# Router logits of a fused attention and expert kernel: from split float32r matmuls to float32 matmuls in four column groups, and four gathers issued in two steps

## The chip, the cores and the metric

One core of a Trainium2 chip runs the whole kernel in one launch. Its engines are TensorE (PE, with its weight loads shown as PEld), VectorE (DVE), ScalarE (ACT), GpSimd (POOL) and SyncE (SP, which issues most DMAs). The metric is device time in microseconds.

## The reference, cut to what matters

```python
scores = scale * np.matmul(q, k.transpose(0, 1, 3, 2))     # 4 batches, 8 heads, 576 places, 64 wide
scores = np.where(masks, scores, -1e9)                      # heads 0-3 a local band, 4-7 every 32nd place
attn = np.exp(scores - scores.max(-1)); attn /= attn.sum(-1) + 1e-9
x = (attn @ v).transpose(0, 2, 1, 3).reshape(2304, 512)
logits = x @ w_gate + modality_bias[modality_id]            # 8 experts
e_idx = np.argmax(logits, axis=1); gate_w = softmax(logits)[e_idx]
for e in range(8):                                          # each token goes to one expert
    out[e_idx == e] = gate_w * (np.maximum(x[e_idx == e] @ w1[e], 0) @ w2[e])
h = out @ w_in; g = np.where(h > 0, h, np.exp(np.minimum(h, 0)) - 1)
result = g @ w_out
```

The logits decide by argmax where a token goes, so they are computed to float32 accuracy. The matmuls of the two feed-forward stages split each operand into a high and a low part in float32r and add three products.

## The kernel before, in words

The kernel has three stages. Attention takes the first 130 us or so, the expert stage follows, and the dense stage (`w_in`, `w_out`) fills the rest. The order of the instructions on every engine is the order in which the code emits them.

**Attention** runs over 32 steps `n` (`NU`): 4 batches by 4 pairs of heads (`PAIRS = [2, 3, 0, 1]`) by 2 halves. A step of the loop emits work of several steps, so that the engines overlap: the scores of step n (`emit_S`, matmul at L1027, two heads in two row groups of 64 rows of the array), transposes of q and k (`emit_T`, L1002), the transposed probabilities of step n-2 (`emit_PT`, L1053), the values of step n-3 (`emit_PV`, L1084, one float32 matmul per piece), the transposed result of step n-5 (`emit_X`, L1121), and the exponentials of step n-1 on ACT (`emit_exp`, L1045). For the masks DVE reads the scores out of PSUM (L1033 or L1038) and takes the row maximum; POOL subtracts the maximum (L1041); then ACT can take the exponentials. The two score banks of PSUM (tag "S") are used again in the next step, so PE's scores of step n+1 wait for DVE's masks of step n.

**The logits.** `emit_X` puts x^T into SBUF in two float32r tiles: ACT casts the high part `xh` (L1129), DVE subtracts it from the PSUM tile for the low part `xl` (L1132). The weight `wgs` holds the high and low parts of `w_gate` side by side, 16 columns (L975, L976). Once all four pairs of a half batch are there, `emit_L` multiplies its 288 places: 4 pieces of the contraction, each with `xh` and with `xl`, eight matmuls of 128 by 16 weights and 288 columns (L1141, L1142) into one bank. There are eight such blocks, six in the attention loop and two in the expert stage. `emit_lg` turns the 16 rows of logits back to places on partitions by nine PE transposes (L1148), and DVE adds the bias and the two halves (L1149, L1150). It runs twice: for the first half of the places in step 21, for the second half in the expert stage. The bias itself is made in step 14 by `emit_bias`: PE transposes the modality numbers, DVE copies them (`m1`, L982; `m0`, L983), POOL forms the bias (L985 to L987), and then `router.constants()` emits a dozen small POOL instructions (iotas, memsets and selects, L214 to L227).

**The first job.** Once the first half of the logits is known, a background generator (`early`) picks the fullest expert among the first 1,152 places, makes a table of its rows and starts its job while attention still runs. The loop calls `bg()` at points between DVE's instructions; a yield of `STEP` holds the generator until the loop's next step. One of its pieces issues four gathers (L460), indirect DMAs on the POOL queue that fetch 128 rows of x each; `scale` (L464) and `trans` (L475) use them some steps later.

Of the kernel before, what the change touches and what calls it, by code (L numbers as in the profile page):

```python
# [8 lines left out]
F32 = mybir.dt.float32  # L9
F32R = mybir.dt.float32r  # L10
# [405 lines left out]
def ffn(tc, ctx, x_dram, part_dram, ident, router, conv, bank, w1, w2, out, run_attention):  # L416
# [187 lines left out]
    def early():  # L604
        STEP = Background.STEP
        yield from router.choose(0, NE)
        yield STEP
        yield from router.early(r_p, lambda: fetch_to(0), lambda: fetch_to(1))
        for c in range(4):
            gather(jobs[0], c)  # L610
            yield STEP if c == 3 else None
        split_to(0)
        fetch_to(2)
        yield STEP
        split_to(1)
        fetch_to(3)
        yield
        for c in range(4):
            scale(jobs[0], c)
            yield STEP if c % 2 else None  # L620
        for kk in range(2):
            trans(jobs[0], kk)
            yield STEP
# [236 lines left out]
def attention(tc, bg, q, k, v, mod, mbias, wg, x_dram, ident, router, bank):  # L860
# [97 lines left out]


    wgf = const.tile([128, 4, E], F32, name="wgf")  # L960
    wgs = const.tile([128, 4, 2 * E], F32R, name="wgs")
    mi = const.tile([NT, 128, 2], I32, name="mi")
    mf = const.tile([NT, 128], F32, name="mf")
    bb = const.tile([128, 2, E], F32, name="bb")
# [1 line left out]
    m0 = const.tile([128, NT], F32, name="m0")  # L966
    bias = const.tile([128, NT, E], F32, name="bias")
    bt = const.tile([128, NT, E], F32, name="bt")
    def load_router():
        nc.scalar.dma_start(wgf, wg.rearrange("(k p) e -> p k e", p=128))  # L970
        nc.scalar.dma_start(mi, mod.bitcast(I32).rearrange("(i p two) -> i p two", p=128, two=2))
        nc.scalar.dma_start(bb, mbias.rearrange("m e -> (m e)").partition_broadcast(128).rearrange("p (m e) -> p m e", m=2))

    def emit_wgs():
        nc.scalar.copy(wgs[:, :, 0:E], wgf)  # L975
        nc.vector.tensor_tensor(wgs[:, :, E:2 * E], wgf, wgs[:, :, 0:E].bitcast(F32), ALU.subtract)  # L976
        nc.vector.tensor_copy(mf, mi[:, :, 0])

    def emit_bias():
# [5 lines left out]
        nc.gpsimd.tensor_tensor(bt, m0.unsqueeze(2).to_broadcast(sh), bb[:, 0:1].to_broadcast(sh), ALU.mult)  # L985
        nc.gpsimd.tensor_tensor(bias, m1.unsqueeze(2).to_broadcast(sh), bb[:, 1:2].to_broadcast(sh), ALU.mult)
        nc.gpsimd.tensor_tensor(bias, bias, bt, ALU.add)  # L987
        router.constants()

    st = {}  # L990
# [65 lines left out]

    xs, stores = {}, []

    xh, xl = (xt_p.tile([128, 4, S], F32R, name=nm) for nm in ("xh", "xl"))
    lgt = const.tile([2 * E, 2 * S], F32, name="lgt")  # L1060

    def emit_PV(n):
        b, pr, s = steps[n]
# [50 lines left out]
    def emit_X(n):  # L1114
# [11 lines left out]
                return t.rearrange("p (m a) -> p a m", a=G)[:, 4 * s:4 * s + 4]  # L1126
            return t.rearrange("p (i m) -> p i m", m=m)[:, nj * s:nj * s + nj]

        nc.scalar.copy(view(xh), ps)  # L1129
        while stores:  # L1130
            stores.pop()(nc.scalar if n + LX < NU else nc.sync)
        nc.vector.tensor_tensor(view(xl), ps, view(xh).bitcast(F32), ALU.subtract)  # L1132
        bg()
        bg()

    def emit_L(b, half):

        ps = bank("T", "ps_l", 2 * E, S // 2)
        c = slice(half * (S // 2), (half + 1) * (S // 2))
        for j, kk in enumerate(PAIRS):  # L1140
            nc.tensor.matmul(ps, lhsT=wgs[:, kk], rhs=xh[:, kk, c], start=j == 0, stop=False)  # L1141
            nc.tensor.matmul(ps, lhsT=wgs[:, kk], rhs=xl[:, kk, c], start=False, stop=j == 3)  # L1142
        nc.scalar.copy(lgt[:, b % 2 * S + c.start:b % 2 * S + c.stop], ps)

    def emit_lg(i0, i1):
        ps = bank("T", "ps_g", 128, i1 - i0, 2 * E)
        for i in range(i0, i1):
            nc.tensor.transpose(ps[:, i - i0], lgt[:, i % NE * 128:(i % NE + 1) * 128], ident[0:2 * E, 0:2 * E])  # L1148
        nc.vector.tensor_tensor(lg[:, i0:i1], ps[:, :, 0:E], bias[:, i0:i1], ALU.add)  # L1149
        nc.vector.tensor_tensor(lg[:, i0:i1], lg[:, i0:i1], ps[:, :, E:2 * E], ALU.add)  # L1150

    for j in range(4):
        emit_T(0, j)
# [67 lines left out]
```

## Time and profile before

| | |
|---|---|
| median of 3 runs | 785.39 us (781.82 to 787.17) |
| the profiled execution's own time | 784.26 us |
| its span, first to last instruction | 782.5 us |
| PE busy | 762.0 us, 97% of the span |
| DVE, ACT, POOL busy | 509.4, 395.9, 103.2 us |
| mean granted TensorE clock | 0.998 |

A busy time counts an instruction from its start to its end, and overlapping matmuls once. The end of a matmul is modelled, so that in a run of matmuls one starts well before the end that is shown for the one before it, and the difference of two starts tells what a matmul costs. In a timeline, consecutive instructions of the same kind are merged into a row with their count; the row's duration reaches from the first start to the last end. A bracket shows idle time of the engine ahead of the row and what ended it. A float32 matmul stands in the trace as two matmul records (two passes over the moving columns), a transpose or a float32r matmul as one.

### The profile page before, as it was taken

To read this page: it belongs to the slowest core of one execution; us is meant where nothing else is said; L and a number is where in the kernel's file an instruction comes from. 1 tells how busy PE (TensorE), PEld (TensorE's weight loads), DVE (VectorE), ACT (ScalarE), POOL (GpSimd) and SP (SyncE) were. 2 spreads that over 40 slices of the span, in tenths; PEclk is the share of its full clock that TensorE was granted. 3 is DMA by queue.
4 is the path that set the end of the run, shared out by engine and by line. 5 is a ranking of instruction groups with operands and counts; after the bars stand their busy time and mean duration, and the time that the engine had idled before them with its cause. 6 is when DMAs were issued, how large, how long until landed. Compare 5 with 4: busy or idle time off the path is not lost.

```text
span 782.5 us, 12469 instructions
## 1 busy us (share of the span) xinstructions
PE 762.0 (97%) x4513; PEld 634.9 (81%) x4513; DVE 509.4 (65%) x1122; ACT 395.9 (51%) x759; POOL 103.2 (13%) x131
## 2 busy tenths in 40 slices
PE   7999989999999999999999999999999999999995
PEld 6999877888888888888787888888888888888885
DVE  4688898776879777677477565664565454545453
ACT  4567566424444444545466455555465444444342
POOL 4335352121020010000000000001010020101011
PEclk9999999999999999999999999999999999999999
DMA  7887591456475666553422221113132030201111
GB/s 162 176 197 179 125 247 58 138 163 204 162 265 171 205 232 199 184 185 118 124 95 91 85 95 41 52 57 121 40 127 89 0 108 1 94 14 52 56 41 67
DMA packets 100300, 94.35 MB, mean 121 GB/s; under 512 B 45433, under 2 KB 78731, under 8 KB 100235
## 3 DMA queue, kind: packets, MB, share of 16 engines
q1 hardware_dynamic: 90880, 74.66, 32.7%
q0 software_dynamic: 4480, 14.68, 5.3%
q10 hardware_dynamic: 4875, 4.17, 1.9%
q8 instruction: 37, 0.61, 0.3%
q14 instruction: 28, 0.23, 0.1%
HBM read 70.95 MB, written 22.54 MB: 119 GB/s over the span
## 4 chain that ended last, share of the span: by engine, by line
PE 44%; DVE 4%; ACT 3%; issue 0%; POOLq 0%; POOL 0%; DVEq 0%; ACTq 0%
PE o_ps L819 8%; PE o_ps L820 7%; PE o_ps L821 7%; PE h_ps L732 7%; PE h_ps L731 7%; PE h_ps L733 7%; DVE r L796 1%; DVE t L795 1%; DVE wl L481 1%; ACT gh L797 1%; ACT wh L480 1%; ACT t L792 0%; ACT e L793 0%; DVE cv_r L158 0%; ACT cv_a L146 0%
## 5 line engine op out<-in xcount | busy, mean ns | idle before, releaser
L795 DVE SCALAR_TENSOR_TENSOR t<-e,t 128x512 f32<-128x512 f32 (+1 forms) x80 | 51.1, 639 | 112.7 <-ACT e L793 112.6
L731 PE MATMUL h_ps<-xh,wh 128*128 128x512 f32 (+1 forms) x320 | 118.6, 371 | 1.3 <-PEq L745 1.3
L732 PE MATMUL h_ps<-xl,wh 128*128 128x512 f32 (+1 forms) x320 | 118.6, 371 | 0.2 <-DVE xl L469 0.2
L733 PE MATMUL h_ps<-xh,wl 128*128 128x512 f32 (+1 forms) x320 | 118.6, 370 | 0.0
L819 PE MATMUL o_ps<-wh,gh 128*128 128x512 f32 x288 | 113.4, 394 | 0.7 <-ACT o L828 0.5
L821 PE MATMUL o_ps<-wh,gl 128*128 128x512 f32 x288 | 113.0, 392 | 0.0
L820 PE MATMUL o_ps<-wl,gh 128*128 128x512 f32 x288 | 112.9, 392 | 0.0
L792 ACT ACTIVATE t<-h_ps 128x512 f32<-128x512 f32 (+1 forms) x80 | 44.2, 553 | 102.2 <-PE h_ps L733 95.4
L797 ACT CAST gh<-r 128x512 fp32r<-128x512 f32 (+1 forms) x80 | 46.2, 577 | 81.0 <-DVE r L796 81.0
L798 DVE TENSOR_TENSOR gl<-r,gh 128x512 fp32r<-128x512 f32 (+1 forms) x80 | 51.2, 640 | 51.4 <-ACT gh L797 51.4
L481 DVE TENSOR_TENSOR wl<-wraw,wh 128x1024 fp32r<-128x1024 f32 x56 | 68.6, 1224 | 14.3 <-ACT wh L480 12.7
L731 PEld LDWEIGHTS h_ps<-xh,wh 128*128 128x128 f32 x320 | 60.2, 188 | 13.4 <-issue 1.7
L732 PEld LDWEIGHTS h_ps<-xl,wh 128*128 128x128 f32 x320 | 60.3, 188 | 12.4 <-DVE xl L469 0.6
L733 PEld LDWEIGHTS h_ps<-xh,wl 128*128 128x128 f32 x320 | 60.1, 188 | 10.9
L819 PEld LDWEIGHTS o_ps<-wh,gh 128*128 128x128 f32 x288 | 54.2, 188 | 13.6 <-ACT o L828 0.9
L516 PE MATMUL y_ps<-hh,wh 128*128 128x512 f32 x160 | 64.2, 401 | 0.0
L821 PEld LDWEIGHTS o_ps<-wh,gl 128*128 128x128 f32 x288 | 54.0, 188 | 12.5 <-DVE gl L798 0.4
L497 PE MATMUL h_ps<-xh,wh 128*128 128x512 f32 x160 | 63.6, 398 | 0.0
L820 PEld LDWEIGHTS o_ps<-wl,gh 128*128 128x128 f32 x288 | 54.1, 188 | 11.1
L499 PE MATMUL h_ps<-xh,wl 128*128 128x512 f32 x160 | 62.9, 393 | 0.0
L518 PE MATMUL y_ps<-hh,wl 128*128 128x512 f32 x160 | 62.8, 393 | 0.0
L498 PE MATMUL h_ps<-xl,wh 128*128 128x512 f32 x160 | 62.8, 392 | 0.0
(180 smaller groups left out, 1380.9 us busy)
## 6 DMA issues: line engine op xcount, KB each, us to landing
wraw<-in_moe_w_dram SPq DMA_DIRECT2D x80, 256.0 KB
raw<-in_moe_w_in_dram SPq DMA_DIRECT2D x16, 512.0 KB
raw<-in_moe_w_out_dram SPq DMA_DIRECT2D x16, 512.0 KB
w_f<-cv_r SPq DMA_DIRECT2D x32, 256.0 KB
wraw<-w_f SPq DMA_DIRECT2D x16, 512.0 KB
part_dram<-o POOLq DMA_DIRECT2D x18, 256.0 KB, 2.9
part<-part_dram SPq DMA_DIRECT2D x18, 256.0 KB
qn<-in_q_dram SPq DMA_DIRECT2D x8, 288.0 KB
```

The lines of the kernel that those rows point to most:

```text
L481: nc.vector.tensor_tensor(WL[i], raw, WH[i].bitcast(F32), ALU.subtract)
L497: nc.tensor.matmul(ps, lhsT=a, rhs=job.xh[kk], start=kk == 0, stop=False)
L498: nc.tensor.matmul(ps, lhsT=a, rhs=job.xl[kk], start=False, stop=False)
L499: nc.tensor.matmul(ps, lhsT=b, rhs=job.xh[kk], start=False, stop=kk == 3)
L516: nc.tensor.matmul(ps, lhsT=a, rhs=hh, start=f == 0, stop=False)
L518: nc.tensor.matmul(ps, lhsT=b, rhs=hh, start=False, stop=f == NCH - 1)
L731: nc.tensor.matmul(ps[:, 0:n], lhsT=a, rhs=yh, start=kk == 0, stop=False)
L732: nc.tensor.matmul(ps[:, 0:n], lhsT=a, rhs=yl, start=False, stop=False)
L733: nc.tensor.matmul(ps[:, 0:n], lhsT=b, rhs=yh, start=False, stop=kk == 3)
L819: nc.tensor.matmul(ps, lhsT=a, rhs=WH[i][:, 512:1024], start=first, stop=False)
L820: nc.tensor.matmul(ps, lhsT=a, rhs=WL[i][:, 512:1024], start=False, stop=False)
L821: nc.tensor.matmul(ps, lhsT=b, rhs=WH[i][:, 512:1024], start=False, stop=last)
```

## The change

The logits are multiplied in float32. `emit_X` copies x^T once, unsplit, to `xt`; `xl` and its subtraction are gone. The weight `wgs` is now 32 columns wide, `w_gate` four times side by side, written by four POOL copies. `emit_L` issues four matmuls, one per piece of the contraction, each to another group of 32 PSUM partitions (another group of 32 columns of the array), so the four partial sums stay apart; ACT copies 128 rows in place of 16. `emit_lg` adds the four up: nine float32 matmuls whose weights are 128 by 128 pieces of the copied logits and whose moving operand is a small constant `sel` (128 by 8, a one where the partition number modulo 32 is the expert's). DVE's second addition (L1150) is gone. `sel` is made in `emit_bias`, by a POOL iota and three DVE instructions, ahead of `router.constants()`. In `early` the step now ends after the second gather in place of the fourth.

```diff
--- before.py
+++ after.py
@@ -608,7 +608,7 @@
         yield from router.early(r_p, lambda: fetch_to(0), lambda: fetch_to(1))
         for c in range(4):
             gather(jobs[0], c)
-            yield STEP if c == 3 else None
+            yield STEP if c == 1 else None
         split_to(0)
         fetch_to(2)
         yield STEP
@@ -958,7 +958,7 @@
 
 
     wgf = const.tile([128, 4, E], F32, name="wgf")
-    wgs = const.tile([128, 4, 2 * E], F32R, name="wgs")
+    wgs = const.tile([128, 4, 32], F32, name="wgs")
     mi = const.tile([NT, 128, 2], I32, name="mi")
     mf = const.tile([NT, 128], F32, name="mf")
     bb = const.tile([128, 2, E], F32, name="bb")
@@ -966,14 +966,16 @@
     m0 = const.tile([128, NT], F32, name="m0")
     bias = const.tile([128, NT, E], F32, name="bias")
     bt = const.tile([128, NT, E], F32, name="bt")
+    sel_i = const.tile([128, E], I32, name="sel_i")
+    sel = const.tile([128, E], F32, name="sel")
     def load_router():
         nc.scalar.dma_start(wgf, wg.rearrange("(k p) e -> p k e", p=128))
         nc.scalar.dma_start(mi, mod.bitcast(I32).rearrange("(i p two) -> i p two", p=128, two=2))
         nc.scalar.dma_start(bb, mbias.rearrange("m e -> (m e)").partition_broadcast(128).rearrange("p (m e) -> p m e", m=2))
 
     def emit_wgs():
-        nc.scalar.copy(wgs[:, :, 0:E], wgf)
-        nc.vector.tensor_tensor(wgs[:, :, E:2 * E], wgf, wgs[:, :, 0:E].bitcast(F32), ALU.subtract)
+        for i in range(32 // E):
+            nc.gpsimd.tensor_copy(wgs[:, :, i * E:i * E + E], wgf)
         nc.vector.tensor_copy(mf, mi[:, :, 0])
 
     def emit_bias():
@@ -985,6 +987,11 @@
         nc.gpsimd.tensor_tensor(bt, m0.unsqueeze(2).to_broadcast(sh), bb[:, 0:1].to_broadcast(sh), ALU.mult)
         nc.gpsimd.tensor_tensor(bias, m1.unsqueeze(2).to_broadcast(sh), bb[:, 1:2].to_broadcast(sh), ALU.mult)
         nc.gpsimd.tensor_tensor(bias, bias, bt, ALU.add)
+
+        nc.gpsimd.iota(sel_i, pattern=[[-1, E]], base=32, channel_multiplier=1)
+        nc.vector.tensor_scalar(sel_i, sel_i, 31, None, ALU.bitwise_and)
+        nc.vector.tensor_copy(sel, sel_i)
+        nc.vector.tensor_scalar(sel, sel, 0.0, None, ALU.is_equal)
         router.constants()
 
     st = {}
@@ -1056,8 +1063,8 @@
 
     xs, stores = {}, []
 
-    xh, xl = (xt_p.tile([128, 4, S], F32R, name=nm) for nm in ("xh", "xl"))
-    lgt = const.tile([2 * E, 2 * S], F32, name="lgt")
+    xt = xt_p.tile([128, 4, S], F32, name="xt")
+    lgt = const.tile([128, 2 * S], F32, name="lgt")
 
     def emit_PV(n):
         b, pr, s = steps[n]
@@ -1126,28 +1133,26 @@
                 return t.rearrange("p (m a) -> p a m", a=G)[:, 4 * s:4 * s + 4]
             return t.rearrange("p (i m) -> p i m", m=m)[:, nj * s:nj * s + nj]
 
-        nc.scalar.copy(view(xh), ps)
+        nc.scalar.copy(view(xt), ps)
         while stores:
             stores.pop()(nc.scalar if n + LX < NU else nc.sync)
-        nc.vector.tensor_tensor(view(xl), ps, view(xh).bitcast(F32), ALU.subtract)
         bg()
         bg()
 
     def emit_L(b, half):
 
-        ps = bank("T", "ps_l", 2 * E, S // 2)
+        ps = bank("T", "ps_l", 128, S // 2)
         c = slice(half * (S // 2), (half + 1) * (S // 2))
         for j, kk in enumerate(PAIRS):
-            nc.tensor.matmul(ps, lhsT=wgs[:, kk], rhs=xh[:, kk, c], start=j == 0, stop=False)
-            nc.tensor.matmul(ps, lhsT=wgs[:, kk], rhs=xl[:, kk, c], start=False, stop=j == 3)
+            o = 32 * (j % 4)
+            nc.tensor.matmul(ps[o:o + 32], lhsT=wgs[:, kk], rhs=xt[:, kk, c], start=j < 4, stop=j >= 4 - 4)
         nc.scalar.copy(lgt[:, b % 2 * S + c.start:b % 2 * S + c.stop], ps)
 
     def emit_lg(i0, i1):
-        ps = bank("T", "ps_g", 128, i1 - i0, 2 * E)
+        ps = bank("T", "ps_g", 128, i1 - i0, E)
         for i in range(i0, i1):
-            nc.tensor.transpose(ps[:, i - i0], lgt[:, i % NE * 128:(i % NE + 1) * 128], ident[0:2 * E, 0:2 * E])
-        nc.vector.tensor_tensor(lg[:, i0:i1], ps[:, :, 0:E], bias[:, i0:i1], ALU.add)
-        nc.vector.tensor_tensor(lg[:, i0:i1], lg[:, i0:i1], ps[:, :, E:2 * E], ALU.add)
+            nc.tensor.matmul(ps[:, i - i0], lhsT=lgt[:, i % NE * 128:(i % NE + 1) * 128], rhs=sel, start=True, stop=True)
+        nc.vector.tensor_tensor(lg[:, i0:i1], ps, bias[:, i0:i1], ALU.add)
 
     for j in range(4):
         emit_T(0, j)
```

On DVE, at the end of step 14 and the first rows of step 15, before (the maxima and values of step 11, the modality numbers, then the masks of step 15):

```order
L1092 RECIPROCAL rs<-rs 72x8 [waits DVE_49]
L1097 TENSOR_TENSOR xs<-ps_v,rs 72x2x128 [waits DVE_49]
L1097 TENSOR_TENSOR xs<-ps_v,rs 72x2x128
L982 COPY m_223<-pm 128x18 [waits PE_49]
L983 TENSOR_SCALAR m_224<-m_223 128x18 [waits DVE_49]
L1038 ISA sm,mx<-ps_sc_1160,mask_l 96x128 [waits PE_49,Pool_49]
L1038 ISA mx 96x1
```

and now:

```order
L1099 RECIPROCAL rs<-rs 72x8 [waits DVE_49]
L1104 TENSOR_TENSOR xs<-ps_v,rs 72x2x128 [waits DVE_49]
L1104 TENSOR_TENSOR xs<-ps_v,rs 72x2x128
L984 COPY m_223<-pm 128x18 [waits PE_49]
L985 TENSOR_SCALAR m_224<-m_223 128x18 [waits DVE_49]
L992 TENSOR_SCALAR sel_i<-sel_i 128x8 [waits Pool_49]
L993 CAST sel<-sel_i 128x8 [waits DVE_49]
L994 TENSOR_SCALAR sel<-sel 128x8 [waits DVE_49]
L1045 ISA sm,mx<-ps_sc_1149,mask_l 96x128 [waits PE_49,Activation_49]
L1045 ISA mx 96x1
```

Three instructions for `sel` now stand between the modality numbers and the masks, and the first of them waits for POOL's iota, which stands behind the three bias instructions on POOL.

On POOL, around step 27 (`sm` is the subtraction of the maximum, `xg` a gather of the first job), before:

```order
L1041 TENSOR_TENSOR sm<-sm,mx 72x576
L400 TENSOR_TENSOR A<-oa,vals 128x180
L1041 TENSOR_TENSOR sm<-sm,mx 72x576 x2
L460 DMA xg<-x_dram,idx 128x512 x4
L1041 TENSOR_TENSOR sm<-sm,mx 72x576
L1041 TENSOR_TENSOR sm<-sm,mx 96x768 x4
```

and now:

```order
L1048 TENSOR_TENSOR sm<-sm,mx 72x576
L400 TENSOR_TENSOR A<-oa,vals 128x180
L1048 TENSOR_TENSOR sm<-sm,mx 72x576 x2
L460 DMA xg<-x_dram,idx 128x512 x2
L1048 TENSOR_TENSOR sm<-sm,mx 72x576
L460 DMA xg<-x_dram,idx 128x512 x2
L1048 TENSOR_TENSOR sm<-sm,mx 96x768 x4
```

Two of the four gathers moved behind the subtraction of step 27 (the one of 72x576 between them).

## Rows read from the trace of the kernel before

**Rows 1.** The page, its first line: span of the profiled execution.

```profile
span 782.5 us, 12469 instructions
```

**Rows 2.** Busy time by stretch: PE, PEld, DVE, ACT, POOL, clock, DMA.

```profile
40.00:60.00 20.00, 20.00 (x278) 18.43 (x278) 16.42 (x71) 13.54 (x38) 7.52 (x6) 1.00 0.79 190
140.00:160.00 20.00, 20.00 (x116) 15.74 (x114) 16.63 (x55) 6.45 (x11) 1.98 (x5) 1.00 0.40 120
```

**Rows 3.** Timeline of PE, a logits block: start, us, line, operands, count.

```profile
51.13 0.35 PE L1141 MATMUL ps_l<-xh,wgs 128*16 128x288 f32 x1
...
52.10 0.29 PE L1142 MATMUL ps_l<-xl,wgs 128*16 128x288 f32 x1
52.23 0.41 PE L1121 MATMUL ps_x<-ident,xs 96*128 96x96 f32 x3
```

**Rows 4.** Timeline of PE, a score block, cut at 53.70, 53.85 and whole.

```profile
53.61 0.35 PE L1027 MATMUL ps_sc<-kt,qt 64*96 64x128 f32 x2
53.61 0.46 PE L1027 MATMUL ps_sc<-kt,qt 64*96 64x128 f32 x4
53.61 0.90 PE L1027 MATMUL ps_sc<-kt,qt 64*96 64x128 f32 x12
```

**Rows 5.** Timeline of PE: two value blocks, what follows one, a turning block.

```profile
52.48 1.20 PE L1084 MATMUL ps_v<-vs,pt 128*72 128x65 f32 x16
...
63.72 1.18 PE L1084 MATMUL ps_v<-vl,pt 128*96 128x65 f32 x12
64.82 0.74 PE L1027 MATMUL ps_sc<-kt,qt 64*72 64x72 f32 x16
...
86.63 0.73 PE L1148 MATMUL ps_g<-ident,lgt 16*128 16x16 f32 x9
87.29 0.35 PE L1027 MATMUL ps_sc<-kt,qt 64*96 64x128 f32 x2
```

**Rows 6.** Groups by line: the low part's subtraction on DVE.

```profile
L1132 DVE TENSOR_TENSOR xl<-ps_x,xh 128x288 fp32r<-128x288 f32 x32 | 18.2, 570 | 8.2 <-ACT xh L1129 7.7
```

**Rows 7.** Timeline of DVE around the bias, step 14.

```profile
61.18 0.70 DVE L1132 TENSOR_TENSOR xl<-ps_x,xh 128x288 fp32r<-128x288 f32 x1 [0.34 <-ACT xh L1129]
...
63.14 0.18 DVE L983 TENSOR_SCALAR m<-m 128x18 f32<-128x18 f32 x1
63.25 0.29 DVE L1038 CUSTOM_DVE_ANT_0 sm<-ps_sc,mask_l 96x128 f32<-96x128 f32 x1
...
64.52 0.08 DVE L1038 DVE_READ_ACCUMULATOR2_ANT mx<- 96x1 f32 x1
```

**Rows 8.** Timeline of POOL around the bias.

```profile
63.40 0.43 POOL L985 TENSOR_TENSOR bt<-m,bb 128x144 f32<-128x144 f32 x1 [0.92 <-DVE m L983]
...
64.74 0.14 POOL L214 IOTA rev<- 128x8 f32 x1
```

**Rows 9.** Timeline of PE, blocks that came late; idle and releaser in brackets.

```profile
69.69 0.72 PE L1053 MATMUL ps_p<-ident,sm 96*128 96x96 f32 x6 [0.64 <-ACT sm L1045]
...
95.99 0.73 PE L1027 MATMUL ps_sc<-kt,qt 64*72 64x72 f32 x14 [0.28 <-DVE mx L1038]
...
101.64 1.20 PE L1084 MATMUL ps_v<-vl,pt 128*96 128x65 f32 x12 [0.25 <-PE ps_x L1121]
...
103.62 1.01 PE L1027 MATMUL ps_sc<-kt,qt 64*72 64x72 f32 x16 [0.78 <-DVE sm L1033]
...
117.59 0.69 PE L1053 MATMUL ps_p<-ident,sm 72*72 72x72 f32 x8 [1.44 <-ACT sm L1045]
...
118.82 0.31 PE L1141 MATMUL ps_l<-xh,wgs 128*16 128x288 f32 x1 [0.28 <-ACT kt L1007]
...
131.39 0.66 PE L475 MATMUL x_ps<-ident,xg 128*128 128x128 f32 x4 [1.18 <-DVE xl L469]
```

**Rows 10.** Timeline of POOL: first of four gathers, what follows the last.

```profile
109.33 1.19 POOL L460 DMA_INDIRECT xg<-x_dram,idx  x1 [0.50 <-DMA vl<-in_v_dram]
...
115.67 2.58 POOL L1041 TENSOR_TENSOR sm<-sm,mx 72x576 f32<-72x576 f32 x2
```

## Prediction

> **What bounds the kernel now.** I read the page first: 782.5 us of span [rows 1] in an execution of 784.26 us, which is 1.1 us under the median of the three runs; the sum below is made against 784.26. Then the busy times by stretch [rows 2]: PE is busy for all of 20.00 us out of 20 both inside attention and where the expert stage begins, at a granted clock of 1.00, while DVE has 3 to 4 us to spare, ACT 6 and more, POOL 12 and more. So a microsecond of PE work that is added or taken away is a microsecond of the kernel, and work of DVE, ACT or POOL counts only where PE waits for it. Then the timeline of PE by starts, since the ends are modelled: what a block of matmuls costs is the distance to the start of the next block. Last the places at which PE came late, with the engine it waited for [rows 9]. The dense stage is not touched; it begins earlier or later by what attention and the first part of the expert stage gain or lose.
>
> **Logits blocks on PE.** Now eight float32r matmuls run one behind the other: 52.23 - 51.13 = 1.10 us from the first to the next block [rows 3]. There are eight such blocks, all where PE is the bound: 8.8 us. In their place come four float32 matmuls, each in two passes. What a pass costs is seen at the scores, which are float32 too: the count rises from 2 to 4 records while the row grows from 0.35 to 0.46 us [rows 4], so a pass of 128 columns takes 0.11 us, and one of 288 columns 0.11 x 288 / 128 = 0.25 us. The same rows show that two tiles of the array run at once: in the first 0.09 us both records are first passes of the two row groups, and each later step of 0.11 us adds one pass of each. The trace has no four column groups, so I bound the block from both sides. If all four run at once, it takes two passes, 0.50 us. If none does, eight passes, 2.0 us. Nothing excludes either end. The nearest rows are the scores, with two independent groups, so I take two passes, and 0.1 us for entering: all twelve passes of the scores reach from first start to last end 0.90 us [rows 4], 0.24 us more than six steps of 0.11, and part of this is only the modelled tail. That is 0.60 us for a block: 8 x (0.60 - 1.10) = **-4.0 us** (ends -4.8 and +7.2).
>
> **Turning the logits back.** Nine transposes took 87.29 - 86.63 = 0.66 us [rows 5]. Nine float32 matmuls come in their place, 18 passes, with 128 weight columns for 8 moving ones, so the weights set the pace. The value blocks show it: with 72 weight columns 16 passes take 53.61 - 52.48 = 1.13 us [rows 4, 5], 0.071 us each; with 96 weight columns 12 passes take 64.82 - 63.72 = 1.10 us, 0.092 us each [rows 5]; both move 65 columns. Another 32 weight columns are 0.028 us more: 0.12 us a pass, 2.2 us a block, +1.5 us. It happens twice, once in attention and once in the expert stage where PE never rests: **+3.0 us** (+2.4, if 0.15 us of each value block is the way to the next block, which makes a pass 0.10 us; +3.1 in proportion to the 96 columns, 0.123 us). This takes back three quarters of the first term.
>
> **The subtraction on DVE.** 32 instructions of 570 ns, 18.2 us, go [rows 6], with one addition in each turning of the logits and one for `wgs`. ACT copies as many elements as it cast. This pays only where PE waited for DVE. From 95 to 104 us, while the routing of the first half runs on DVE, PE stood idle 0.28, 0.25 and 0.78 us [rows 9]; a bracket starts at a modelled end, and without a wait the scores at 64.82 start 0.08 us before the end of the row ahead (63.72 + 1.18 = 64.90) [rows 5], so each is some 0.1 us more: 1.6 us. Each of these steps loses one subtraction, 0.57 us, and the turning that is 1.5 us longer lets DVE catch up as well; I expect these waits to go, and some tenths of shorter ones beside them: **-2.0 us** (0, or -2.6 with 1.0 us of shorter ones). At 131.39 PE waited 1.18 us for a split of the first job's x, behind two steps of the same chain over DVE, POOL and ACT [rows 9]; one subtraction in that chain is 0.6 us: **-0.6 us** (0 to -1.2).
>
> **The gathers.** Four gathers hold POOL from 109.33 to 115.67 us [rows 10], and the subtraction of the maximum of step 27 stands behind them; so its exponentials were late, PE waited 1.44 us at 117.59, and again 0.28 us at 118.82 because ACT was late with the copy after them [rows 9]. With two gathers ahead of it, half of 6.3 us, the subtraction starts near 112.5 and ends before 114 (two of them take 2.58 us [rows 10]), early enough. What is late next: the other two gathers now hold up step 28's subtraction, to about 117; in the kernel before it began at 115.67 + 2.58 / 2 = 117 too. The rows are gathered one step later, but split and scaled in the same steps as before. 1.44 + 0.28 and 0.1 for each modelled end: **-2.0 us** (0, or -2.4 if the scores behind start earlier too).
>
> **A wait that is added.** `sel` needs POOL's iota, which stands behind three bias instructions, and DVE stands still for it with the masks of step 15 behind. POOL began the bias at 63.40 and its next iota at 64.74 [rows 8]. DVE is some 0.35 us earlier there (its subtraction at 61.18 [rows 7] is gone), so the iota ends at 64.74 + 0.14 - 0.35 = 64.5. Three small DVE instructions, 0.2 us each with what lies between, put the masks at 65.2 in place of 63.25; they take 64.60 - 63.25 = 1.35 us [rows 7] and end at 66.5. PE's next scores use the same banks and started at 64.82 [rows 5]: they come 1.7 us late. At 69.69 PE had waited 0.64 us for exponentials that were late behind POOL's constants [rows 9]; that wait is covered now. Net **+1.0 us** (0 to +1.7). The four POOL copies for `wgs` fit into POOL's idle time, 12 us in 20 [rows 2], and come three steps before the first block; if they came late, the first block alone would wait.
>
> **Sum.** -4.0 + 3.0 - 2.0 - 0.6 - 2.0 + 1.0 = -4.6 us: 784.26 - 4.6 = **779.7 us**.
>
> **Rivals.**
> *The column groups take turns by program order.* Each matmul is a first and a second pass; the second cannot start before the first is through, and if the next group's first pass may not overtake it, a block needs five slots of 0.25 us, first, three shared ones, last: 1.35 us with the entry, 8 x 0.25 = +2.0 in place of -4.0, so 785.7 us. For it: the four groups use the same 128 rows, unlike the scores' row groups. Against it: at the scores the second row group's first pass did start ahead of the first one's second [rows 4]. The Trainium skill (TensorE: Matmul & The Clock Gate, the part on packing small matmuls) states this order: matmuls start and end in program order, and weights load over running matmuls only where the row groups differ. By that rule the time is this rival's; rows 4 do not agree with it for row groups, and no run here shows column groups. The skill's page TensorEngine Tiling (Array Packing), key properties, says that tiles work independently, which gives the forecast. Chance 0.20.
> *The column groups do not overlap at all* (slower): the moving columns of four float32 streams are read one after the other, from the first block at 51 us. A block is eight passes, 2.1 us: +8.0 in place of -4.0, 791.7 us. From 1.18 us a block on, the change costs time. For it: the trace shows no two matmuls over the same rows at once. Chance 0.12.
> *The late starts stay,* because POOL or ACT is late next where DVE was: only -4.0 + 3.0 + 1.0 are left, 784.3 us. For it: at 117.59 and 131.39 the chain goes over three engines [rows 9]. Chance 0.08.
> *More is gained:* blocks at 0.50 us, all late starts at their ends and the new wait hidden: -4.8 + 3.0 - 2.6 - 1.2 - 2.4 = -8.0, 776.3 us. Chance 0.08.
>
> **Numbers.** The forecast itself, 779.7 us, has 0.52; its own range is 777 to 782.5. The range of 775.5 to 788 leaves out the case without overlap (0.12) and the outer ends of the rest. 1%, about what a measurement of this kernel can tell from no change, is 7.8 us: faster than that needs most of the last rival or a lucky forecast, 0.14; slower needs the case without overlap and another loss, 0.05; within it 0.81.
>
> **What would show it.** The distance from the first logits matmul to the next block: 0.6 us forecast, 1.35 by turns, 2.1 without overlap. The turning block: 2.2 us for 18 passes. No idle bracket of PE for ACT near 117 us, none for DVE between 95 and 104. A new wait of PE for DVE at the scores of step 16, near 66 us, and DVE idle for POOL's iota just before. I am wrong if the dense stage's own blocks change, or if PE begins to wait for weights once attention is shorter.

## The result: slower, and outside the range

| kernel | time, median (range) | against the kernel before, 95% interval |
|---|---|---|
| before | 785.33 us (781.82 to 787.17) | |
| the change | 793.14 us (792.94 to 793.85) | 1.0112 (1.0090 to 1.0135) |

The forecast was 779.7 us in a range of 775.5 to 788.0. The kernel became 7.8 us slower (four executions of each); slower by more than 1% had a chance of 0.05. The profiled execution took 792.94 us, with a span of 791.2 us [rows 1].

The page of the changed kernel: span, busy times, and the granted clock in 40 slices of 19.8 us (9 is 90% or more of full speed).

```profile
span 791.2 us, 12489 instructions
...
PE 771.3 (97%) x4531; PEld 642.7 (81%) x4531; DVE 497.9 (63%) x1090; ACT 398.2 (50%) x758; POOL 104.4 (13%) x136
...
PEclk9996789999999999999999999999999999999998
```

DVE lost 11.5 us of work, PE gained 9.3 us, and the clock row has a dip in slices 4 to 6 (6, 7, 8). I cut attention where the clock changes. Columns: stretch, its length, busy time of PE, PEld, DVE, ACT and POOL with instructions, granted clock, DMA share, GB/s.

```profile
24.40:65.30 40.90, 39.40 (x554) 35.81 (x553) 29.39 (x153) 28.81 (x70) 19.60 (x32) 1.00 0.83 188
65.40:85.80 20.40, 20.40 (x165) 19.65 (x163) 8.70 (x22) 10.83 (x24) 5.25 (x5) 0.50 0.53 126
85.90:96.00 10.10, 10.10 (x128) 8.56 (x127) 6.16 (x38) 5.63 (x14) 2.94 (x2) 1.00 0.46 118
96.10:102.80 6.70, 6.70 (x60) 6.41 (x62) 4.00 (x26) 2.99 (x7) 2.52 (x6) 0.50 0.06 14
```

PE is busy for the whole of both half-clock stretches, so its busy time alone would not show that anything is wrong. It gets through 165 matmuls in 20.40 us, where the 40.90 us ahead of them hold 554. Before, the clock stayed at 1.00 in the same two stretches of time, and the first of them held 271 matmuls:

```profile
65.40:85.80 20.40, 19.76 (x271) 18.18 (x268) 16.42 (x63) 13.72 (x38) 10.01 (x16) 1.00 0.81 192
96.10:102.80 6.70, 6.45 (x89) 5.97 (x89) 6.39 (x29) 4.80 (x13) 2.62 (x2) 1.00 0.66 189
```

PE's timeline at the places of the forecast (start, us, operation, count, and in brackets the idle time ahead and what ended it):

```profile
49.58 0.69 PE L1148 MATMUL ps_l<-xt,wgs 128*32 128x288 f32 x8
50.20 0.47 PE L1128 MATMUL ps_x<-ident,xs 96*128 96x96 f32 x3
...
61.23 1.18 PE L1091 MATMUL ps_v<-vl,pt 128*96 128x65 f32 x12
63.68 0.32 PE L1034 MATMUL ps_sc<-kt,qt 64*72 64x72 f32 x2 [1.27 <-DVE mx L1045]
64.22 0.73 PE L1034 MATMUL ps_sc<-kt,qt 64*72 64x72 f32 x14 [0.23 <-DVE mx L1045]
...
66.98 2.12 PE L1091 MATMUL ps_v<-vl,pt 128*96 128x65 f32 x12
69.03 1.24 PE L1034 MATMUL ps_sc<-kt,qt 64*72 64x72 f32 x16
...
93.89 2.13 PE L1154 MATMUL ps_g<-sel,lgt 128*128 128x8 f32 x18
95.95 1.54 PE L1034 MATMUL ps_sc<-kt,qt 64*96 64x128 f32 x12
...
113.03 1.01 PE L1034 MATMUL ps_sc<-kt,qt 64*72 64x72 f32 x16 [0.79 <-DVE sm L1040]
...
129.57 0.46 PE L1034 MATMUL ps_sc<-kt,qt 64*96 64x128 f32 x2 [0.75 <-DVE mx L1045]
```

The logits block is 0.62 us long (50.20 - 49.58; 1.10 in [rows 3]), the turning 2.06 us (95.95 - 93.89; 0.66 in [rows 5]). PE waits 1.27 and 0.23 us for the masks, where it did not wait at 64.82 [rows 5]. Soon after, the same value block takes 2.05 us (69.03 - 66.98), where at full clock it took 1.10 [rows 5]. The wait of 1.44 us at 117.59 [rows 9] is gone, the one of 0.78 at 103.62 is still there (113.03), and a new one of 0.75 us stands at 129.57, for masks.

The wait of DVE behind it, and what POOL did meanwhile:

```profile
60.34 0.18 DVE L985 TENSOR_SCALAR m<-m 128x18 f32<-128x18 f32 x1
62.12 0.29 DVE L992 TENSOR_SCALAR sel_i<-sel_i 128x8 int32<-128x8 int32 x1 [1.60 <-POOL sel_i L991]
...
62.82 0.39 DVE L1045 CUSTOM_DVE_ANT_0 sm<-ps_sc,mask_l 96x128 f32<-96x128 f32 x1
```

```profile
61.50 0.49 POOL L989 TENSOR_TENSOR bias<-bias,bt 128x144 f32<-128x144 f32 x1
61.95 0.13 POOL L991 IOTA sel_i<- 128x8 int32 x1
```

This is the added wait as forecast: iota behind the bias, DVE still for it, masks at 62.82 instead of right behind 60.34, PE's scores late by 1.5 us in all.

### The profile page after: what moved, and what is told of

The parts are those of the page before. It is cut to its first block, busy times and chain, and to the rows that moved or that the text cites. A ratio compares the mean times of both kernels' runs of the same rounds, so it can differ in the third digit from the quotient of the medians.

```text
span 791.2 us, 12489 instructions
## 1 busy us (share of the span) xinstructions
PE 771.3 (97%) x4531; PEld 642.7 (81%) x4531; DVE 497.9 (63%) x1090; ACT 398.2 (50%) x758; POOL 104.4 (13%) x136
## 4 chain that ended last, share of the span: by engine, by line
PE 44%; DVE 3%; ACT 3%; issue 0%; POOLq 0%; POOL 0%; DVEq 0%; ACTq 0%
PE o_ps L819 7%; PE o_ps L821 7%; PE o_ps L820 7%; PE h_ps L732 7%; PE h_ps L731 7%; PE h_ps L733 7%; DVE r L796 1%; DVE t L795 1%; DVE wl L481 1%; ACT gh L797 1%; ACT wh L480 1%; ACT t L792 0%; ACT e L793 0%; DVE cv_r L158 0%; ACT cv_a L146 0%
```

## The experiments

Two theories. **A:** the added wait is what costs, by bringing PE's clock down, and the other terms came about as forecast. **B:** the logits matmuls or the turning themselves cost the time (their shapes, or the clock they leave behind).

**Sel made early.** The iota goes to step 2, the three DVE instructions to step 9, where DVE has room. Nothing else changes.

```diff
     def load_router():
+        nc.gpsimd.iota(sel_i, pattern=[[-1, E]], base=32, channel_multiplier=1)
...
     def emit_wgs():
+        nc.vector.tensor_scalar(sel_i, sel_i, 31, None, ALU.bitwise_and)
+        nc.vector.tensor_copy(sel, sel_i)
+        nc.vector.tensor_scalar(sel, sel, 0.0, None, ALU.is_equal)
```

> The changed kernel, with the constant for the turning made early: its iota on POOL in step 2, its three DVE instructions in step 9, so that DVE never stands still for POOL in step 14. Theory A (PE's wait of 1.3 us for the masks at step 16, which this iota causes, is what brings the granted clock down at 65 us): no idle bracket of 1.27 us at the scores of step 16, granted clock 1.00 from 24 to 85 us, and the time falls from 793 to 778-782 us; a second, short fall right behind the turning block near 85-90 us may remain, and would cost 2 to 4 us. Theory B (the logits blocks themselves, in column groups, leave PE with too little work, and the wait is a bystander): the clock falls near 65 us as before, time 791-793 us. Either way the four logits blocks cost 0.6 us each and the turning block 2.1 us.

Measured: 777.95 us (777.82 to 781.65), 0.9939 (0.9918 to 0.9959) of the kernel before, which took 783.79 us there. Its windows and PE's rows:

```profile
65.40:85.80 20.40, 20.07 (x271) 17.82 (x268) 13.99 (x59) 13.24 (x34) 7.45 (x6) 1.00 0.76 183
85.90:140.00 54.10, 51.33 (x597) 44.29 (x595) 43.92 (x183) 36.00 (x80) 20.35 (x20) 1.00 0.57 153
```

```profile
60.63 1.18 PE L1090 MATMUL ps_v<-vl,pt 128*96 128x65 f32 x12
61.74 0.74 PE L1033 MATMUL ps_sc<-kt,qt 64*72 64x72 f32 x16
...
99.14 1.01 PE L1033 MATMUL ps_sc<-kt,qt 64*72 64x72 f32 x16 [0.96 <-DVE sm L1039]
```

No wait at the scores, no half clock, 271 matmuls in the stretch that held 165. The logits and the turning are the same as in the changed kernel, so B falls for the main loss. The shorter half-clock stretch behind the turning (96.10 to 102.80 in the change) is absent here too, with the same turning; what brings it stays open. This version is faster than both kernels, by 0.6% than the one before.

**The wait alone,** in the kernel before: the iota and the three DVE instructions in step 14, their result unused.

```diff
         nc.gpsimd.tensor_tensor(bias, bias, bt, ALU.add)
+        nc.gpsimd.iota(sel_i, pattern=[[-1, E]], base=32, channel_multiplier=1)
+        nc.vector.tensor_scalar(sel_i, sel_i, 31, None, ALU.bitwise_and)
+        nc.vector.tensor_copy(sel, sel_i)
+        nc.vector.tensor_scalar(sel, sel, 0.0, None, ALU.is_equal)
```

> The kernel before, with only the iota and the three DVE instructions put into step 14 as the change does (their result is not used). Theory A: PE waits 1 us or more at the scores of step 16, the granted clock falls near 65-70 us for some 20 us, time 790-796 us, 5 to 10 us over the kernel before. Theory B: the wait costs what it is long, +0.5 to +1.7 us, the clock stays at 1.00.

Measured: 793.78 us (792.60 to 794.25), 1.0123 (1.0103 to 1.0144).

```profile
63.53 0.32 PE L1033 MATMUL ps_sc<-kt,qt 64*72 64x72 f32 x2 [1.54 <-DVE mx L1044]
64.08 0.80 PE L1033 MATMUL ps_sc<-kt,qt 64*72 64x72 f32 x14 [0.23 <-DVE mx L1044]
```

```profile
64.70:88.40 23.70, 23.70 (x187) 22.46 (x186) 13.50 (x37) 10.82 (x24) 5.83 (x5) 0.50 0.52 128
```

Four small instructions, 10 us. Neither the logits nor the gathers are needed for the long stretch at half clock.

**The gathers alone,** in the kernel before (`c == 3` becomes `c == 1`).

> The kernel before, with only the gathers issued two and two. By the prediction's term: PE's idle of 1.44 us at 117.59 and of 0.28 at 118.82 go, time -2.0 us (0 to -2.4), about 783. The rival (late starts stay, because another engine is late next): same time within 0.5 us, and a new bracket in place of the old one.

Measured: 781.95 us (780.96 to 784.95), 0.9985 (0.9973 to 0.9998): 1.8 us by the medians, with an interval from near nothing to 2.1. PE's late scores near 117 now:

```profile
118.15 0.46 PE L1027 MATMUL ps_sc<-kt,qt 64*96 64x128 f32 x2 [0.48 <-DVE mx L1038]
118.78 0.89 PE L1027 MATMUL ps_sc<-kt,qt 64*96 64x128 f32 x10 [0.18 <-DVE mx L1038]
```

The wait of 1.44 us for exponentials [rows 9] is gone, and 0.48 us of waiting for masks came in its place. In the two profiled executions little is left for the gathers: the same PE instructions start 2.6 us earlier at 30 us already, because the clock rose 6.5 us earlier at the start, 3.05 us earlier at 130 and 2.7 us at 200. So the two traces give 0.2 to 0.5 us, and the forecast's 2.0 us is within the interval but not shown.

**The logits alone,** sel early, four gathers in one step.

> The kernel with sel made early (777.95 us where it was timed, 5.8 under the kernel before), with the four gathers back in one step as before. Theory (the sum's terms add up): what is left is the logits alone, L blocks -4.0, turning +2.9, VectorE's late starts -2.0, the wait at 131 us -0.6 = -3.7 against the kernel before, that is 2 us above the kernel with sel early. Rival (the split of the gathers only pays once the logits are changed, or the other way round): within 1 us of the kernel with sel early, or of the kernel before.

Measured: 780.94 us (780.04 to 782.22), 0.9959 (0.9940 to 0.9978), 4.1 us by the medians under the kernel before, which took 785.00 there. By the medians the two parts add up (1.8 + 4.1 against 5.8), within wide intervals. The traces speak more for the rival, that the split of the gathers pays mainly once the logits are changed. With all four gathers in one step PE waited longer than in the kernel before, and the clock fell there too:

```profile
111.87 1.19 PE L1147 MATMUL ps_l<-xt,wgs 128*32 128x288 f32 x8 [2.89 <-ACT qt L1011]
```

```profile
111.80:115.00 3.20, 3.13 (x24) 2.22 (x25) 2.33 (x14) 2.54 (x8) 0.86 (x1) 0.50 1.06 337
```

Against sel early the same PE instructions are 1.14 us later at 106 us and 3.58 us later at 117: 2.4 us for the gathers in one step, in one execution of each.

**A shorter wait.** In the changed kernel, the iota is moved ahead of all three bias operations on POOL, or ahead of the last one. The three DVE instructions stay where they are.

```diff
+        nc.gpsimd.iota(sel_i, pattern=[[-1, E]], base=32, channel_multiplier=1)
         nc.gpsimd.tensor_tensor(bt, ...)
         nc.gpsimd.tensor_tensor(bias, ...)
         nc.gpsimd.tensor_tensor(bias, bias, bt, ALU.add)
-        nc.gpsimd.iota(sel_i, pattern=[[-1, E]], base=32, channel_multiplier=1)
```

> The changed kernel with one instruction moved: the iota of sel's numbers is issued on GpSimd ahead of the three bias operations instead of behind them; the three VectorE operations on them stay in step 14. In the changed kernel VectorE waited 1.60 us for that iota (until 62.12 us) and TensorE 1.27 us for the masks behind it. Theory A (the wait of TensorE brings the clock down, not the added work): the wait of VectorE is gone, its three operations take some 0.7 us, TensorE waits under 0.3 us for the masks, the granted clock stays at 1.00, and the time is that of the experiment with sel made early, 778 us (777 to 780). Rival B (some 0.7 us of VectorE work at this place is enough to bring the clock down): half clock from about 65 us for 20 us as in the changed kernel, 788 to 793 us.

> The changed kernel with the iota of sel's numbers between the second and the third of the three bias operations on GpSimd, so that VectorE's wait is shorter by the third one's 0.45 us. TensorE's wait for the masks comes to about 0.8 us instead of 1.27. Theory A' (the clock only falls from a wait about as long as the one seen): granted clock 1.00 throughout, 778 plus 0.8 = 779 us. Rival C (at this place any added wait of that kind brings the clock down): half clock from about 65 us, 788 to 793 us.

Measured, iota first: 780.17 us (778.27 to 784.16). DVE and PE:

```profile
59.93 0.17 DVE L991 TENSOR_SCALAR sel_i<-sel_i 128x8 int32<-128x8 int32 x1
...
60.87 0.28 DVE L1044 CUSTOM_DVE_ANT_0 sm<-ps_sc,mask_l 96x128 f32<-96x128 f32 x1
```

```profile
61.85 1.16 PE L1033 MATMUL ps_sc<-kt,qt 64*72 64x72 f32 x16
```

The scores are stretched from 0.74 to 1.16 us and no more; the clock stays up in all of attention. Some 0.9 us of extra DVE work at this place (59.93 to 60.87) costs attention nothing in the profile: the same PE instructions are 0.1 us later than with sel early at 60 us and level with it at 100. So it is the wait that hurts. The median is a little above the 777 to 780 us that were expected. Iota in the middle, in the profiled execution:

```profile
64.63 0.32 PE L1033 MATMUL ps_sc<-kt,qt 64*72 64x72 f32 x2 [0.92 <-ACT sm L1051]
65.18 0.73 PE L1033 MATMUL ps_sc<-kt,qt 64*72 64x72 f32 x14 [0.23 <-DVE mx L1044]
```

Its twelve times fall into two groups: six of 780.8 to 784.1 us at a mean granted clock of 0.992 to 0.994, and six of 789.5 to 794.2 us at 0.978 to 0.982. So each of the two expected outcomes came, roughly, in half of the executions (the first 2 to 5 us above its 779), and neither theory of a fixed outcome holds for this length of wait. The bracket puts the wait down to ACT, but PE starts 0.86 us behind the first mask (63.77 us), just as in the change (63.68 behind 62.82).

**The wait filled.** The changed kernel as it is, with seven unused matmuls of the identity with itself ahead of step 16's scores. DVE and POOL are as late as in the changed kernel, but PE works.

```diff
     for n in range(NU):
+        if n == 16:
+            ps = bank("T", "ps_f", 128, 128)
+            for i in range(7):
+                nc.tensor.matmul(ps, lhsT=ident, rhs=ident, start=i == 0, stop=i == 6)
         emit_S(n)
```

> The changed kernel as it is, late masks and all, with seven unused float32 matmuls of 128x128 by 128x128 (fourteen passes of about 0.11 us, 1.5 us) put on TensorE just ahead of the scores of step 16, where it waited 1.27 us: the wait stays as long, but TensorE works through it. Theory A (it is TensorE standing idle there that brings the clock down): clock 1.00 through the attention up to the turning, and the time is that with sel early plus the 1.5 us of the filled wait, 779.5 us (779 to 783; 3.4 more if the clock still falls behind the turning, as it did with two column groups). Rival (something else in the late chain, on VectorE or GpSimd, brings it down): half clock from about 65 us for 20 us as in the changed kernel, 792 to 795 us.

Measured: 782.46 us (781.01 to 785.67), 0.9986 (0.9969 to 1.0003), where the changed kernel took 793.14.

```profile
62.91 0.29 DVE L992 TENSOR_SCALAR sel_i<-sel_i 128x8 int32<-128x8 int32 x1 [1.60 <-POOL sel_i L991]
```

```profile
63.05 1.78 PE L1163 MATMUL ps_f<-ident 128*128 128x128 f32 x14
64.75 1.00 PE L1034 MATMUL ps_sc<-kt,qt 64*72 64x72 f32 x16
```

```profile
22.50:87.10 64.60, 63.97 (x882) 58.22 (x880) 46.46 (x228) 44.36 (x111) 28.30 (x38) 1.00 0.82 190
87.30:94.00 6.70, 6.70 (x60) 6.38 (x61) 3.72 (x25) 3.00 (x7) 2.52 (x6) 0.50 0.08 20
```

Adding 1.7 us of useless work to the bounding engine made the kernel some 10 us faster. That is the strongest evidence for A: the chain over POOL and DVE is unchanged (DVE still waits 1.60 us for POOL), only PE's standing still is gone. What separates its profile from that of sel early is 1.3 us of the filled wait, 2.5 us of a short fall behind the turning, 1.4 us at the start and 0.9 us at a wait between the expert and the dense stage, which is taken up below.

**The wait at other places.** The kernel with sel early, and a pause of the same make (two DVE, three POOL instructions, an iota, three DVE instructions that wait for it, all unused) at the end of step 6, 10 or 22.

```diff
+        if n == 6:      # or 10, or 22
+            pause()
```

> Sel made early, and a pause of the same make as the changed kernel's (two VectorE operations, three GpSimd operations on 128x144, an iota, three VectorE operations that wait for it; their results are unused) put at the end of step 10, some 10 us ahead of where it stood. The masks of step 11 come late and TensorE waits about 1 us for them in the scores of step 12 or 13. Theory A (in this stretch of small matmuls any such wait of TensorE brings the clock down): a stretch at half clock of some 20 us from about 46 us on, 787 to 794 us. Rival B (it hung on the place in step 16): clock 1.00, 778 to 780 us.

> The same pause at the end of step 22 instead, where the steps have the same shapes as step 14 but VectorE also has the routing's work. Theory A: TensorE waits over 1 us for the masks in the scores of step 24 or 25 and the clock falls to half from about 93 us on, 787 to 794 us. Rival B: clock 1.00, 778 to 780 us.

> The same pause at the end of step 6, the place with the same shapes in the first batch, some 10 us after the clock has come up to full. Theory A: TensorE waits over 1 us in the scores of step 8 and the clock falls to half from about 35 us on, 787 to 794 us. Rival B: clock 1.00, 778 to 780 us.

PE behind the pause at step 10, 22 and 6, each with the half-clock stretch behind it:

```profile
49.00 1.26 PE L1047 MATMUL ps_sc<-kt,qt 64*96 64x128 f32 x12 [1.27 <-DVE sm L1053]
```

```profile
50.80:57.40 6.60, 6.60 (x50) 5.07 (x49) 3.07 (x20) 2.84 (x7) 2.08 (x2) 0.50 0.47 115
```

```profile
93.75 0.42 PE L1047 MATMUL ps_sc<-kt,qt 64*72 64x72 f32 x2 [2.29 <-DVE mx L1058]
```

```profile
94.00:117.70 23.70, 23.49 (x198) 22.41 (x198) 14.01 (x54) 11.77 (x25) 9.68 (x9) 0.50 0.64 159
```

```profile
36.53 0.32 PE L1047 MATMUL ps_sc<-kt,qt 64*72 64x72 f32 x2 [1.29 <-DVE mx L1058]
```

```profile
38.90:59.20 20.30, 20.30 (x165) 19.43 (x165) 9.32 (x28) 9.83 (x23) 5.18 (x8) 0.50 0.63 151
```

All runs that bear on the wait, ordered by the length that the added wait of PE has in the profiled execution. A mean clock of 0.984 or less marks a long fall; all other executions of these kernels have 0.989 or more, which leaves room for short ones:

| kernel | PE's added wait, us | time, median (range), us | executions at a mean clock of 0.984 or less |
|---|---|---|---|
| sel early | none | 777.95 (777.82 to 781.65) | 0 of 6 |
| iota first | none, scores 0.42 longer | 780.17 (778.27 to 784.16) | 0 of 12 |
| wait filled | none, 1.7 of added work | 782.46 (781.01 to 785.67) | 0 of 12 |
| iota in the middle | 0.92 + 0.23 | 786.77 (780.82 to 794.15) | 6 of 12 |
| pause at step 10 | 1.27 | 782.22 (779.64 to 786.02) | 0 of 10 |
| the change | 1.27 + 0.23 | 793.14 (792.94 to 793.85) | 4 of 4 |
| pause at step 6 | 1.29 + 0.23 | 792.71 (781.63 to 795.38) | 6 of 10 |
| wait alone in the kernel before | 1.54 + 0.23 | 793.78 (792.60 to 794.25) | 4 of 4 |
| pause at step 22 | 2.29 + 0.21 | 790.14 (783.22 to 791.55) | 9 of 10 |
| logits alone (a wait for ACT, gathers in one step) | 2.89 | 780.94 (780.04 to 782.22) | 0 of 9 |

Steps 6, 14 and 22 have the same shapes, and the clock falls behind each, so the place in step 16 is nothing special. The pause at step 22 is the least clean of them, since it stands some 8 us behind the turning, which was followed by falls of its own in other runs. At step 10 the profiled execution, the slowest of the ten, has a fall of 6.6 us only, and the expected 787 to 794 did not come. So the long fall differs from execution to execution of one kernel. It is not equally likely at every step, and the length of the wait alone does not decide it: behind the longest one, 2.89 us, the profile has 3.4 us at half clock, and none of nine executions has a long fall. What decides it in one execution stays open.

**Two column groups** instead of four, sel early.

```diff
-            o = 32 * (j % 4)
-            nc.tensor.matmul(ps[o:o + 32], ..., start=j < 4, stop=j >= 4 - 4)
+            o = 32 * (j % 2)
+            nc.tensor.matmul(ps[o:o + 32], ..., start=j < 2, stop=j >= 2)
```

> Sel made early, gathers two by two, and the logits in two column groups of the array instead of four: each group then takes two of the four pairs, one after the other, and the results lie in 64 rows. Theory (the column groups run at once, and a block takes its passes per group): a block has four passes of 0.247 us per group instead of two, about 1.1 us against 0.62; over 8 blocks +3.9 us against the 777.95 us with four groups, 781.9 us (780.5 to 783). The turning of 9 tiles stays at about 2.06 us. Rival (the block's length is set by issue and weight loads, not by the passes): blocks of 0.6 to 0.7 us and 778 us.

```profile
51.40 1.16 PE L1147 MATMUL ps_l<-xt,wgs 128*32 128x288 f32 x8
52.50 0.47 PE L1127 MATMUL ps_x<-ident,xs 96*128 96x96 f32 x3
```

The block takes 1.10 us against 0.62, as expected: passes of different groups run at once, passes of one group follow each other. The time, 784.58 us (783.22 to 786.25), is 6.6 above the kernel with sel early instead of 3.9. In the two profiled executions, whose spans are 8.0 us apart, the starts of the same instructions drift by 0.47 us at each of the eight blocks (3.8 us); another 2.4 us are the clock's rise at the start, 5.0 us later, and 2.8 us a fall of 6.8 us behind the turning. Later waits are together some 1.0 us shorter. The expected 780.5 to 783 us had no such fall in it.

**The turning by transposes,** sel early: 128x128 transposes in place of float32 matmuls with `sel`, the four groups added up by DVE. The first four tiles of each half are also turned some steps earlier, which the diff below does not show.

```diff
-            nc.tensor.matmul(ps[:, i - i0], lhsT=lgt[...], rhs=sel, start=True, stop=True)
-        nc.vector.tensor_tensor(lg[:, i0:i1], ps, bias[:, i0:i1], ALU.add)
+            nc.tensor.transpose(ps[:, i - i0], lgt[...], ident)
+        nc.vector.reduce_sum(lg[:, i0:i1], ps.rearrange("p i (g c) -> p i c g", g=4)[:, :, 0:E], axis=AX.X)
+        nc.vector.tensor_tensor(lg[:, i0:i1], lg[:, i0:i1], bias[:, i0:i1], ALU.add)
```

> Sel made early, gathers two by two, and the turning of the logits done by 18 transposes of 128x128 (one pass each) with VectorE adding up the four groups in PSUM, in parts of 2 to 4 tiles, instead of 18 float32 matmuls with sel (two passes each); the first four tiles of each half are turned some steps earlier. Theory (TensorE is the bound, the turning counts at its length): 9 transposes take about 9 x 0.10 = 0.9 to 1.0 us against 2.06, twice 1.1 = 2.2 us less than 777.95, 775.7 us (775 to 777). Rival (six additions over 128x(2 to 4)x32 from PSUM on VectorE make the masks late again): 777 to 779 us, with waits of TensorE for VectorE behind the turning.

```profile
82.88 0.71 PE L1153 MATMUL ps_g<-ident,lgt 128*128 128x128 f32 x5
83.52 0.90 PE L1033 MATMUL ps_sc<-kt,qt 64*96 64x128 f32 x12
...
88.21 0.89 PE L1033 MATMUL ps_sc<-kt,qt 64*96 64x128 f32 x10 [0.18 <-DVE mx L1044]
```

Measured: 778.88 us (777.08 to 780.29), 0.9948 (0.9929 to 0.9966), not to be told from sel early. Compared with that kernel, the scores behind the turning began 1.1 us earlier (83.52 against 84.62), but by 93.9 us PE was 0.2 us later. The routing on DVE did not become shorter: the next masks began at 86.83 us in one and 86.81 in the other, and PE waited for them. So in attention the longer turning of sel early had been hidden behind the routing. In the expert stage PE was 0.8 us earlier (139.59 against 140.38), and had lost it by 373 us: 0.4 us at 154, and as much at the wait between the two stages (1.60 us against 1.16). The expected 775 to 777 us did not come, the rival's 777 to 779 did.

## Why the prediction was wrong

**The step that failed** is the term "A wait that is added". It had the chain right, instruction by instruction, and its length nearly (1.27 + 0.23 us of wait against 1.7), and it priced the wait at its length. Every other term, too, was made at the clock of [rows 2], and no rival had a clock that falls. Between the changed kernel and the one with sel early, which differ in nothing else, the starts of the same PE instruction drift apart like this:

| at (sel early, us) | the change is later by | what lies between |
|---|---|---|
| 61.1, value block ahead of the scores | 0.6 us | clock up to full speed 1.8 us later at the start |
| 62.4, behind these scores | 2.5 us | the wait, +1.9 |
| 76.2 to 84.6 | 11.3 us | first half-clock stretch, +8.8 |
| 99.1 | 13.9 us | second one, behind the turning, +2.6 |
| 430 and later | 14.9 us | 1.0 more at a wait between the expert and the dense stage, which no edit touches |

So 11.4 of 14.9 us are the two half-clock stretches, and 1.9 the wait. The wait between the stages is in every profile, 1.03 to 2.30 us long, at the branch that asks whether more expert jobs are to run. In the change it is

```profile
387.48 0.47 PE L731 MATMUL h_ps<-xh,wh 128*128 128x512 f32 x1 [2.19 <-PEq L745]
```

and with sel early 1.16 us. The dense stage's own blocks did not change: the distance stays 14.9 us from 430 to 700 us. The trace of before had a hint that I read the other way: waits of 1.44 and 1.18 us stood in it [rows 9] without a fall, and I took waits to cost their length.

**The other terms,** from the same comparison of before with the kernel with sel early:

| term | forecast | measured |
|---|---|---|
| eight logits blocks | -4.0 | -2.3 |
| two turnings | +3.0 | +1.35 and +1.2 |
| DVE's late starts up to 104 us | -2.0 | -2.3 |
| gathers | -2.0 | -0.8 |
| the split at 131 us | -0.6 | -0.8 |
| start: full clock at 22.6 us, before at 27.8 | | -2.3 |

The sum without the wait was -5.6 us, and the medians gave -5.8 (777.95 against 783.79). The agreement is partly luck: in the two profiled executions, which lie 6.2 us apart, 2.3 us come from the start, where no edit is, and the logits blocks gave 1.7 us and the gathers 1.2 us less than forecast.

*Logits blocks.* The block from its first matmul to the next block was right, 0.62 against 0.60 us, and the four groups do run at once; the rivals of turns and of no overlap fall. The starts, from the trace of the kernel with sel early:

```
us       matmul
48.800   L1008 third transpose of q
48.975   L1147 first pass, group 0     (48.981, 48.988, 48.995: groups 1 to 3)
49.241   L1147 second pass, group 0    (49.248, 49.255, 49.261: groups 1 to 3)
49.598   L1127 first transpose of x
```

But the way in and out was missing from the term. In the kernel before, the first logits matmul came 0.03 us behind the last transpose's start; here it comes 0.175 us behind, where two transposes are 0.08 us apart, and the last second passes hold the next block off for 0.34 us, while a pass takes 0.25 to 0.27. From the last transpose to the next block it is 0.80 us against 1.13, and the next block's first step is 0.05 us longer: 0.28 us saved a block, not 0.50. The Trainium skill (TensorEngine Tiling (Array Packing), Key Properties) says that changing the tiling mode drains the engine; these 0.2 us a block agree with it, and I had cited the neighbouring property only. The Trainium skill's other page (TensorE: Matmul & The Clock Gate, the part on packing small matmuls) has weights load over running matmuls only where the row groups differ; the second passes here take the same rows in other column groups and begin 7 ns apart, with the block at the length of two passes, so here that rule does not keep them apart. Their four weight loads start at 49.001 to 49.021 us, while the first passes run.

*Turning.* 2.06 us against 2.2; in its place in attention it added 1.35, part of which the waits for the routing behind it gave back.

*DVE.* The wait of 0.78 us at 103.62 did not go (0.79 at 113.03 in the change, 0.96 at 99.14 with sel early); shorter ones did, so the sum came out. 0.4 us of it is the wait of 0.64 us at 69.69, which the forecast had set against the added wait.

*Gathers.* The exponentials are on time, as said; what became late next was the masks (0.75 us at 129.57), one step further than I had looked. That took back most of the term.

## What to carry to other kernels

Where one engine is the bound and is full of small matmuls, price a new wait of TensorE by what the clock may do, not by its length: four instructions that held it for 1.5 us cost 10 us in the kernel before, and the changed kernel took 15 us more with them than with sel early. Other waits of such a length, in the same traces, had no fall behind them. Make constants where the waiting engine has slack, look at the clock row before the busy times, and remember that a full PE row can be a PE at half speed. A cheap test for a suspected wait is to fill it with useless matmuls: if the kernel becomes faster and the granted clock stays up, it was TensorE's standing still that brought the clock down.

## What was not expected of the hardware

- A single wait of 0.92 to 2.3 us in attention was followed by a clock of 1.2 GHz for 20.3 to 23.7 us (6.6 us at step 10), though PE was busy throughout that stretch (20.40 of 20.40 us in the change). That it was the wait is shown for step 16, by the wait filled. A long fall may or may not come: 6 of 12 executions at 0.92 us, 0 of 10 with 1.27 us at step 10. Other waits had none in their profiles: 1.44 and 1.18 us in the kernel before [rows 9], 0.96 us at 99.14 with sel early. The wait between the expert and the dense stage was followed by 3.4 us at half clock in three profiles (wait alone 1.84 us, iota first 2.06, pause at step 10 2.30), and by none in others (the change 2.19, wait filled 2.09). What tells these cases apart is open, and so is what ends such a stretch. The Trainium skill (TensorE: Matmul & The Clock Gate, A second HAM failure mode) describes short idle stretches, coming often between groups of matmuls, with which the clock goes back and forth between its two levels. These runs agree that short ones can do it; here one wait was enough (4 of 4 executions of the change).
- The kernel before is not free of lower clocks either. Of its 98 executions timed beside the experiments, 14 have a mean granted clock of 0.990 or less (median 786.0 us) and 66 of 0.995 or more (782.8 us); the profiled one has 0.998. Where the clock fell in the others no trace shows.
- The turning, 18 passes that move 8 columns each, was followed by a fall of 3.4 to 6.8 us in the profiles of six kernels (the change, iota in the middle, two groups, pauses at steps 6 and 10, wait filled) and by none in three (sel early, logits alone, iota first). That the turning causes it is not shown by an experiment. The transposes that move 128 columns were followed by none in the one profile.
- The clock first reached full speed between 20.2 and 27.8 us in the fourteen profiles, in no relation to the edits; 5 us there are worth 2.3 to 2.4 us of the kernel's time.
- Entering and leaving four column groups cost 0.2 us a block beyond the passes.
